# Block products of two token blocks in one set: 512 columns each, with an order of their own for h, gates and second products

## The chip, the cores and the metric

The kernel runs on one core of one Trainium2 chip. Its time is the device time of one launch in microseconds (us), the median of several runs; smaller is better.

## The reference, cut to what matters

Sparse attention over 2 batches of 8 heads (768 tokens, 64 wide) gives x, 1536 tokens by 512. Two feed-forward layers follow, and they are most of the work:

```python
def _moe_ref(x, w_in, w_out):          # first layer
    h = x @ w_in                       # 1536x512 @ 512x2048
    g = h * np.cos(h)
    return g @ w_out                   # 1536x2048 @ 2048x512

def _moe2_ref(x, w_in, w_out):         # second layer, on the first one's result
    h = x @ w_in
    relu6 = np.clip(h + 3.0, 0.0, 6.0)
    g = h * relu6 / 6.0
    return g @ w_out
```

All inputs are float32, and so is the result.

## The kernel before, in words

**Precision.** TensorE multiplies in a reduced form of float32. Each operand is therefore split into a high and a low part ("hi", "lo"), and each product is made of three: hi with hi, lo with hi, hi with lo. The weights are split on the chip (carry, rebias, shift, sign, join, then hi and lo, in `nearest`, `convert` and `convert_pair`), and so are x and g.

**Tiling.** The 1536 tokens are three blocks of 512 (0, 1, 2). A feed-forward layer's 2048 inner columns are 16 slices of 128. For a slice and a block there is first h (128 inner columns on the partitions, 512 tokens in the free dimension), then the gate work (`middle`: turns, rest, cosine, gate in the first layer; relu and gate six in the second; then g hi and g lo), then the second product (`mm2`, 12 matmuls of 512 columns) that adds into four accumulator banks in PSUM. After the last slice of a run of slices, `close` adds the four banks into `total` ("sums", on VectorE where the sum is not the first). The slices are worked in groups (`GROUPS`), each group for the three blocks in turn.

**h in two ways.** The slices 0 to 5 of the first layer are computed directly (`mm1`, line 990). All others come two slices at a time from `mm1_set` (line 923, matmuls at line 941): the product of a 2 by 2 weight block matrix with a 2 by 2 token block matrix is formed from seven block products and not eight. The four weight blocks are two slices by two halves of the depth; sums of them (s1 to s4) come from `convert_pair` and lie in `phi`, `plo`. The four token blocks are two halves of the depth by the two halves (256 tokens each) of one token block; sums of them ("tees") come from `tees` and `tees_of_parts` and lie in `tx`. A block product is six matmuls: three parts by two halves of 128 in depth. One set uses three banks x, y and w of a ring of four (`LATE_H`), and moves each product out of PSUM with "take" (a copy, line 521) or "add" (line 954, VectorE) into tiles `hs`. Four times in a set a product goes into a bank that an add (three times) or a take (once) must have read first.

**Order.** The program is recorded as a list of operations with their dependencies (`Graph.op`). `QUEUES`, a table of numbers at the head of the file, gives every operation an engine and a place in the engine's queue; engines work their queues in that order. `Graph.replay` estimates times only to merge the queues and to place filler matmuls (`fill`, line 1078) where PE would be idle. So a new table moves nearly every instruction.

**Names in the rows.** PE: line 941 is a block product, line 990 a direct h product, line 1108 a second product. DVE is VectorE: line 954 add, 1146 sums, 1068 g lo, 1064 gate six, 1055 rest, 1059 gate, 598/600/602 weight conversion, 538 lo parts of the weights, 851/864/869 tees and their lo parts, 1158 low part of the first layer's result. `hs`, `ch_c` hold h and the gate's tiles; `ghi`, `glo` are g; `total`, `totak` the results; `bank_...` are PSUM banks. POOL is GpSimd, ACT is ScalarE.

```python
def product(o, ok, a, t, first=False, wait=0.0):   # before: bh, bl are 256 columns of one block
    ...
    for n, (wt, xt) in enumerate(((phi, bh), (plo, bh), (phi, bl))):
        for kk in range(2):
            nc.tensor.matmul(
                o, wt[i][:, A[a], kk * P:(kk + 1) * P], xt[:, kk, :], ...
```

Of the kernel before, what the change touches and what calls it, by code (L numbers as in the profile page):

```python
# [11 lines left out]
F32 = mybir.dt.float32  # L12
# [20 lines left out]
def wstart(w, seq):  # L33
# [5 lines left out]
        4 18 19 26 27 35 36 77 43 44 52 53 79 66-68 86 87 69-71 103 94 105 82 96 99 112 121 123 114 381 369-371  # L39
        117 393 394 372 373 382 383 395 396 130 374 397 398 384 385 132 386 149 135 151 405 158 439 160 406 440  # L40
        421 407 408 422 409 163 441 410 423 442 443 424 425 176 444 419 167 178 169 426 181 417 420 418 433 457
        434 436 458 200-205 459-462 438 185 211 187 435 437 491 213 492 493 453 494 216 451 454 452 473 495 474
# [3 lines left out]
        566 568 570 286 573 571 574 572 594-597 606-608 598 609 654 599 610 618 611 655 656 619 620 657 621 622  # L46
        658 623 659 678-681 704-707 682 667 683 666 708 709 749 765 750 766 668 751 767 752-754 669 768 691 693
        690 769 695 735 692 770 694 734 733 783 736 784 785 763 786 787 762 788 829 830 761 831 764 777 779 863
        781 778 845 822 780 846 832 821 833 847 782 834 824 848 842 823 849 850 841 857 864 859 865 861 866 867
        907 844 868 843 929 858 860 915 862 908-910 927 931 916 917 953 918 934 954 956 932 955 936 939 957 967  # L50
# [272 lines left out]
def attention_two_ffn(  # L323
# [30 lines left out]
    HALF = TOK // 2  # L354
    NHB = 2
    GROUPS = ((3, 3, 4, 2, 4), (4, 4, 4, 4))
    BACKWARD = ((0, 0, 0, 1, 1), (1, 0, 1, 0))
    WHOLE = GROUPS[0][0] + GROUPS[0][1]
    plan = []
    for m in range(2):  # L360
# [977 lines left out]
```

## Time and profile before

| | |
|---|---|
| median of 3 runs | 584.77 us (583.97 to 584.91) |
| the profiled execution's own time | 584.38 us |
| span of its trace, first to last instruction | 582.5 us |
| PE busy | 574.1 us (99% of the span), 4303 matmuls in the trace |
| weight loads, DVE, ACT, POOL busy | 508.7, 495.0, 350.6, 209.6 us |
| granted PE clock | 1.000 in the whole span |
| chain that ended last | PE 93%, DVE 4%, DMA, ACT, issue and POOL 1% each |

[...] The attention runs until about 99 us, mixed with the first direct products; from about 100 to 154 us PE has direct and second products alone, and from 154 to 570 us block products and second products; the rest is the last second products and the stores.

### The profile page before, as it was taken

The numbers are of one execution on the slowest core, as the hardware profiler recorded it, in microseconds if no ns is written. First come the engines' busy times: TensorE is split into PE (matmuls) and PEld (weight loads), VectorE is DVE, ScalarE is ACT, GpSimd is POOL, SyncE is SP. The second block draws the span as 40 slices with busy tenths as digits, with TensorE's granted clock in tenths as the row PEclk, the third lists the DMA queues.
The fourth block names the chain that finished last, engine by engine and source line by source line (L and its number), as shares of the span: only waits on it lengthen the run. The fifth ranks groups of instructions, "written<-read, shape, count | busy, mean of one in ns | idle before, by whom it ended". The sixth has DMA issues, their size and how long they took to land.

```text
span 582.5 us, 11210 instructions
## 1 busy us (share of the span) xinstructions
PE 574.1 (99%) x4303; PEld 508.7 (87%) x4303; DVE 495.0 (85%) x975; ACT 350.6 (60%) x768; POOL 209.6 (36%) x203
## 2 busy tenths in 40 slices
PE   9999999999999999999999999999999999999997
PEld 7788889888899888889879898899998989898985
DVE  6998898988988989999899999988988888875644
ACT  5899998777565576757657767754673354231110
POOL 5586655433533342253524531203114004023130
PEclk9999999999999999999999999999999999999999
DMA  8996543212022112331210211321222230200014
GB/s 305 288 279 209 166 145 100 74 36 73 0 74 74 38 71 74 109 109 38 74 36 1 73 58 52 110 73 72 74 73 73 80 109 30 72 1 1 1 55 163
DMA packets 17093, 51.58 MB, mean 89 GB/s; under 512 B 1936, under 2 KB 2192, under 8 KB 17040
## 3 DMA queue, kind: packets, MB, share of 16 engines
q1 hardware_dynamic: 17040, 50.86, 26.2%
q8 instruction: 34, 0.56, 0.4%
q14 instruction: 19, 0.16, 0.1%
HBM read 47.71 MB, written 3.15 MB: 87 GB/s over the span
## 4 chain that ended last, share of the span: by engine, by line
PE 93%; DVE 4%; DMA 1%; ACT 1%; issue 1%; POOL 1%; SPq 0%; DVEq 0%
PE bank_a L1108 24%; PE bank_d L941 17%; PE bank_c L1108 10%; PE bank_b L1108 10%; PE bank_c L941 8%; PE bank_e L941 8%; PE bank_d L990 4%; PE bank_e L990 2%; PE bank_b L793 2%; PE bank_b L809 2%; PE bank_c L990 1%; PE bank_c L730 1%; DMA ktile<-in_kt_dram 1%; PE bank_d L1078 1%; DVE totak L1146 1%; PE bank_c L713 1%
## 5 line engine op out<-in xcount | busy, mean ns | idle before, releaser
L1062 ACT ACTIVATE ch_c<-hs,three 128x512 f32<-128x512 f32 x48 | 34.0, 721 | 64.8 <-DVE hs L954 60.8
L1068 POOL TENSOR_TENSOR glo<-ch_c,ghi 128x512 fp32r<-128x512 f32 x26 | 35.1, 1355 | 74.9 <-ACT ghi L521 33.5
L954 DVE TENSOR_TENSOR hs<-bank_d,hs 128x256 f32<-128x256 f32 x100 | 41.8, 420 | 16.5 <-PE bank_d L941 15.4
L602 POOL TENSOR_TENSOR cv_y<-cv_t,cv_y 128x512 int32<-128x512 int32 x23 | 33.3, 1451 | 58.5 <-DVE cv_t L600 43.4
L521 ACT CAST ghi<-ch_c 128x512 fp32r<-128x512 f32 x63 | 38.9, 620 | 16.0 <-DVE ch_c L1064 8.7
L600 DVE SCALAR_TENSOR_TENSOR cv_t<-raw,cv_t 128x512 int32<-128x512 int32 x64 | 45.1, 705 | 0.2
L1068 DVE TENSOR_TENSOR glo<-ch_c,ghi 128x512 fp32r<-128x512 f32 x58 | 43.1, 746 | 0.7 <-ACT ghi L521 0.6
L593 ACT ACTIVATE cv_t<-raw 128x512 f32<-128x512 f32 x55 | 36.8, 673 | 10.9 <-DVE plo L538 2.9
L583 ACT ACTIVATE cv_y<-raw 128x512 int32<-128x512 uint32 x58 | 38.6, 675 | 5.8 <-DVE wlo_out L538 2.4
L1064 DVE SCALAR_TENSOR_TENSOR ch_c<-ch_c,hs 128x512 f32<-128x512 f32 x48 | 33.2, 698 | 3.7 <-ACT ch_c L1062 3.6
L1053 ACT ACTIVATE ch_c<-hs,quarter 128x512 int32<-128x512 f32 x30 | 21.4, 722 | 21.6 <-DVE hs L954 18.7
L1057 ACT ACTIVATE ch_c<-ch_c,half_pi 128x512 f32<-128x512 f32 x37 | 26.3, 721 | 12.3 <-DVE ch_c L1055 11.9
L941 PE MATMUL bank_d<-xhi,phi 128*128 128x256 f32 x156 | 31.2, 281 | 1.2 <-DVE hs L954 1.2
L941 PEld LDWEIGHTS bank_d<-xhi,phi 128*128 128x128 f32 x156 | 27.2, 189 | 5.5 <-DVE hs L954 1.6
L941 PE MATMUL bank_d<-xhi,plo 128*128 128x256 f32 x156 | 31.4, 282 | 0.0
L941 PE MATMUL bank_d<-xlo,phi 128*128 128x256 f32 x156 | 31.3, 282 | 0.0
L954 DVE TENSOR_TENSOR hs<-bank_e,hs 128x256 f32<-128x256 f32 x47 | 19.8, 421 | 13.3 <-PE bank_e L941 12.8
L598 DVE TENSOR_SCALAR cv_t<-cv_t 128x512 int32<-128x512 int32 x64 | 28.3, 446 | 0.8 <-ACT cv_t L593 0.7
L602 DVE CUSTOM_DVE_ANT_0 cv_y<-cv_t,cv_y 128x1024 uint16<-128x1024 uint16 x41 | 28.6, 705 | 0.3 <-ACT cv_y L583 0.2
L954 DVE TENSOR_TENSOR hs<-bank_c,hs 128x256 f32<-128x256 f32 x48 | 20.1, 418 | 9.1 <-PE bank_c L941 8.6
L763 ACT ACTIVATE es<-bank_c,nmx 128x120 f32<-128x120 f32 x80 | 27.5, 370 | 0.2
L771 POOL TENSOR_TENSOR es<-es,rs 128x960 f32<-128x960 f32 (+1 forms) x13 | 21.4, 1649 | 12.1 <-DVE rs L770 9.9
(367 smaller groups left out, 1978.2 us busy)
## 6 DMA issues: line engine op xcount, KB each, us to landing
raw<-in_w_in_dram SPq DMA_DIRECT2D x32, 512.0 KB, 3.6
raw<-in_w_out_dram SPq DMA_DIRECT2D x32, 512.0 KB, 3.6
vcats<-in_vw_dram SPq DMA_DIRECT2D x12, 384.0 KB, 5.7
qt<-in_q_dram SPq DMA_DIRECT2D x12, 256.0 KB, 5.1
ktile<-in_kt_dram SPq DMA_DIRECT2D x7, 384.0 KB, 5.3
total<-in_vw_dram SPq DMA_DIRECT2D x8, 256.0 KB, 4.9
out_dram<-total SPq DMA_DIRECT2D x8, 256.0 KB, 2.2
vnat<-in_vw_dram SPq DMA_DIRECT2D x4, 256.0 KB, 6.4
```

The source lines that it names most:

```text
L521: nc.scalar.copy(o, i) if e == "ACT" else VEC[e].tensor_copy(o, i)
L583: nc.scalar.activation(y, low.bitcast(U32), AF.Copy, scale=2.0 ** -29)
L593: nc.scalar.activation(o, a, AF.Copy, scale=2.0 ** -112)
L600: G.op("sign", {"DVE": dve(DM)}, lambda e: nc.vector.scalar_tensor_tensor(t, high, -0x80000000, t, ALU.bitwise_and, ALU.bitwise_or), r=[rk ...
L602: G.op("join", {"POOL": pool(DM), "DVE": dve(DM)}, lambda e: VEC[e].tensor_tensor(y, t, y, ALU.add), r=[tk], w=[yk], twice=True)
L941: nc.tensor.matmul(o, wt[i][:, A[a], kk * P:(kk + 1) * P], xt[:, kk, :], start=first and n + kk == 0, stop=n + kk == 3, skip_group_check=True)
L954: G.op("add", {"DVE": dve(HALF)}, lambda e: nc.vector.tensor_tensor(o[0](), a, b[0](), ALU.add), r=[ak, b[1], "room"], w=[o[1]])
L990: nc.tensor.matmul(h, w["in"][i][:, kk * P:(kk + 1) * P], x[blk][:, kk, c0:c1], start=p + kk == 0, stop=p == 2 and kk == NK - 1)
L1062: G.op("relu", {"ACT": act(N) + 0.1}, lambda e: nc.scalar.activation(c(), h(), AF.Relu, bias=three), r=hk, w=ck)
L1064: G.op("gate six", {"DVE": dve(N)}, lambda e: nc.vector.scalar_tensor_tensor(c(), c(), 6.0, h(), ALU.min, ALU.mult), r=hk, w=ck, twice=boo ...
L1068: G.op("g lo", {"DVE": dve(N), "POOL": pool(N)}, lambda e: VEC[e].tensor_tensor(gbuf("lo", s)[:, 0:N], c(), gh().bitcast(F32), ALU.subtrac ...
L1108: nc.tensor.matmul(acc(s, i)[0], l, r, start=first, stop=end and p == 2 and (N == TOK or i % 2 == 1), skip_group_check=N < TOK)
```

## The change

It does five things.

1. The token blocks 0 and 1 are put into one set (`SIDE = [[0, 1], [2]]`): the two columns of the token block matrix are then block 0 and block 1, 512 tokens each (`WIDE = [512, 256]`). Block 2 keeps sets of its own, with halves of 256. All block products, adds and takes of a two-block set work on 512 columns.
2. The sums of token blocks are made for both blocks together, for each 128 of depth in turn (`chunks`), in `tees(0)` after block 1's last result of the first layer and in `tees_of_parts(0, ...)` before the first sets; block 2 has `tees(1)`. The upper half of block 1's result is no longer split by itself, since only sums that contain it are used.
3. From the first set on, an explicit list (`work`) sets what is recorded in which order: a two-block set, the second products left from block 2 of the group before, a second two-block set, then second products and sets of block 2 in turn. The gate work of a slice is recorded as soon as a g tile is free. `BACKWARD`, by which the last block of a group was the first of the next, is gone; with it the four places where a block's accumulators were kept open from one group to the next.
4. h and the gate share one pool of seven tiles (`tile_of`, `assign`).
5. V's block means are copied from PSUM in one operation of four copies, on one engine, and no longer in four operations. The table `QUEUES` is new.

The diff, cut to its core (the table's rows are left out, as are some lines of `tees` that only follow the new indices):

```diff
     GROUPS = ((3, 3, 4, 2, 4), (4, 4, 4, 4))
-    BACKWARD = ((0, 0, 0, 1, 1), (1, 0, 1, 0))
...
-            n = LATE_H[(SETS - NEARLY + (s - SETS) // 2 * 3 + k) % 4]
+            n = LATE_H[(SETS - NEARLY + s - SETS + k) % 4]
+            return bank[n], n
...
+            def put(e):
+                for c in range(P // BLK):
+                    hs = slice(c * CC // D, (c + 1) * CC // D)
+                    copy(e, vcat[0][WK:KC, :, hs, :], bank[mb][BLK * c:BLK * c + NB, 0:CC].rearrange(
+                        "n (h d) -> n h d", d=D).unsqueeze(1).to_broadcast([NB, 2, CC // D, D]))
+
+            G.op("put v", {"ACT": 4 * act(2 * CC), "DVE": 4 * dve(2 * CC)}, put, r=[mb], w=every)
...
+    SIDE = [[0, 1], [2]]
+    WIDE = [TOK, HALF]
+
+    def chunks(z):
+        return (0, 1) if z == 0 else (None,)
+
+    def quarter_of(x, z, k, t, c=None):
+
+        if z == 0:
+            return x[t][:, 2 * k:2 * k + 2, :] if c is None else x[t][:, 2 * k + c, :]
+        return x[SIDE[1][0]][:, 2 * k:2 * k + 2, t * HALF:(t + 1) * HALF]
...
-    def mm1_set(s, due):
+    def mm1_set(z, rows, number, due):
...
-        (x, xk), (y, yk), (w, wk) = (hbank(s, k) for k in range(3))
-        x, y, w = (z[:, 0:HALF] for z in (x, y, w))
+        n = WIDE[z]
+        (x, xk), (y, yk), (w, wk) = (hbank(SETS + 3 * number, k) for k in range(3))
+        x, y, w = (v[:, 0:n] for v in (x, y, w))
...
-            G.op("block product", {"PE": 6 * mm(HALF)}, go, r=[("phi", i, AK[a]), ("plo", i, AK[a]), *xr], w=[ok], due=late[0])
+            G.op("block product", {"PE": 6 * mm(n)}, go, r=[("phi", i, AK[a]), ("plo", i, AK[a]), *xr], w=[ok], due=late[0])
...
         def add(o, a, ak, b):
-            G.op("add", {"DVE": dve(HALF)}, lambda e: nc.vector.tensor_tensor(o[0](), a, b[0](), ALU.add),
-                 r=[ak, b[1], "room"], w=[o[1]])
+            G.op("add", {"DVE": dve(n)}, lambda e: nc.vector.tensor_tensor(o[0](), a, b[0](), ALU.add),
+                 r=[ak, *b[1], "room"], w=o[1])
...
+            z = next(z for z in range(2) if blk in SIDE[z])
+            n = TOK if i >= NK // 2 or blk == SIDE[0][0] else (HALF if z else 0)
...
+            if i == NK - 1 and blk == SIDE[z][-1]:
+                tees(z)
...
+                work += sets(0, pairs[0]) + left
+                if len(pairs) > 1:
+                    work += sets(0, pairs[1])
+                left = seconds(2, range(f0, f0 + n))
+                if m == 0 and f0 + n == NF:
+                    work += seconds(0, range(f0, f0 + n)) + seconds(1, range(f0, f0 + n))
+                    work += [x for f in pairs for x in sets(1, f)] + left
+                    left = []
+                else:
+                    for f in pairs:
+                        work += seconds(0, two(f)) + sets(1, f)
+                    work += seconds(1, range(f0, f0 + n))
```

What it moves is read from the order of instructions in the two programs. First PE in the second half of the second layer's first group, before: block products of 256 columns (two matmuls to a row) between second products of 512.

```order
L1108 MATMUL bank_a0_93<-ghi3_1653,whj_out0_1643 128x512
L1108 MATMUL bank_a0_93<-ghi3_1653,wlj_out0_1645 128x512
L1108 MATMUL bank_a0_93<-glo3_1657,whj_out0_1643 128x512
L1108 MATMUL bank_b_95<-ghi3_1653,whj_out0_1643 128x512
L1108 MATMUL bank_b_95<-ghi3_1653,wlj_out0_1645 128x512
L1108 MATMUL bank_b_95<-glo3_1657,whj_out0_1643 128x512
L1108 MATMUL bank_a1_94<-ghi3_1653,whj_out0_1643 128x512
L1108 MATMUL bank_a1_94<-ghi3_1653,wlj_out0_1645 128x512
L1108 MATMUL bank_a1_94<-glo3_1657,whj_out0_1643 128x512
L941 MATMUL bank_d0_98<-xhi2_87,phi1_70 128x256 x2
L941 MATMUL bank_d0_98<-xhi2_87,plo1_72 128x256 x2
L941 MATMUL bank_d0_98<-xlo2_90,phi1_70 128x256 x2
```

And PE after the change, where the first layer ends and the second layer's first two-block set begins: ten block products of block 2 (256 columns; the last three are shown), the first block product of 512 columns, then second products.

```order
L944 MATMUL bank_d0_98<-xhi2_87,phi0_69 128x256 x2
L944 MATMUL bank_d0_98<-xhi2_87,plo0_71 128x256 x2
L944 MATMUL bank_d0_98<-xlo2_90,phi0_69 128x256 x2
L944 MATMUL bank_d1_99<-xhi2_87,phi0_69 128x256 x2
L944 MATMUL bank_d1_99<-xhi2_87,plo0_71 128x256 x2
L944 MATMUL bank_d1_99<-xlo2_90,phi0_69 128x256 x2
L944 MATMUL bank_c1_97<-xhi2_87,phi0_69 128x256 x2
L944 MATMUL bank_c1_97<-xhi2_87,plo0_71 128x256 x2
L944 MATMUL bank_c1_97<-xlo2_90,phi0_69 128x256 x2
L944 MATMUL bank_e_100<-xhi0_85,phi1_70 128x512 x2
L944 MATMUL bank_e_100<-xhi0_85,plo1_72 128x512 x2
L944 MATMUL bank_e_100<-xlo0_88,phi1_70 128x512 x2
```

In the whole program the 1638 matmuls of 256 columns in block products became 546 of 512 and 546 of 256; the 1080 second products of 512 columns, the direct products and the attention's matmuls are as many as before, and 25 filler matmuls stand where 26 stood, all in the attention.

DVE at the end of the first layer, before: the closing sums of the last block (totak), a weight conversion, the last g lo parts, and the adds (line 954) of a set of the block worked before.

```order
L1146 SCALAR_TENSOR_TENSOR totak0_1658<-bank_b_95,totak0_1658 128x512
L1146 SCALAR_TENSOR_TENSOR totak0_1658<-bank_a1_94,totak0_1658 128x512
L1146 SCALAR_TENSOR_TENSOR totak0_1658<-bank_c0_96,totak0_1658 128x512
L600 SCALAR_TENSOR_TENSOR cv_t1_84<-raw1_68,cv_t1_84 128x512
L1068 TENSOR_TENSOR glo1_1655<-ch_c1_1648,ghi1_1651 128x512
L1158 TENSOR_TENSOR xlo2_90<-totak0_1658,xhi2_87 128x256
L1068 TENSOR_TENSOR glo2_1656<-ch_c2_1649,ghi2_1652 128x512
L954 TENSOR_TENSOR hs0_1665<-bank_d1_99,hs0_1665 128x256
L954 TENSOR_TENSOR hs0_1665<-bank_e_100,hs0_1665 128x256
```

DVE at the same place after the change: the closing sums of block 1, sums of token blocks (line 880) and low parts (line 1179) between the adds (line 960) of the ten block products shown above.

```order
L1165 SCALAR_TENSOR_TENSOR total1_92<-bank_c0_96,total1_92 128x512
L880 TENSOR_TENSOR total1_92<-total1_92 128x512
L960 TENSOR_TENSOR ch_c1_1647<-bank_d1_99,ch_c1_1647 128x256
L960 TENSOR_TENSOR ch_c1_1647<-bank_e_100,ch_c1_1647 128x256
L880 TENSOR_TENSOR total0_91<-total0_91,total1_92 128x512
L960 TENSOR_TENSOR hs1_1663<-bank_d0_98,ch_c0_1646 128x256
L960 TENSOR_TENSOR ch_c1_1647<-bank_d1_99,ch_c1_1647 128x256
L1179 TENSOR_TENSOR xlo1_89<-total1_92,xhi1_86 128x512
L960 TENSOR_TENSOR ch_c0_1646<-bank_d0_98,ch_c0_1646 128x256
L1179 TENSOR_TENSOR xlo1_89<-total1_92,xhi1_86 128x512
L1074 SCALAR_TENSOR_TENSOR hs3_1665<-ch_c1_1647,hs3_1665 128x512
L960 TENSOR_TENSOR ch_c0_1646<-bank_d1_99,ch_c0_1646 128x256
```

After these come the rest of the gate work of block 2's four slices (twelve instructions), sums of token blocks and their low parts (twelve with those shown; three more sums are on POOL), one low part of weights, three steps of weight conversion, two closing sums of block 2, and the first two adds of the two-block set. From the first add shown to the second of these two it is 43 DVE instructions: nine adds of 256 columns, one weight shift, and 33 others of 512. Over the whole program, DVE's adds go from 195 of 256 columns to 65 of 256 and 65 of 512, its sums from 68 to 84, and its other groups change by a few each.

## Rows read from the trace of the kernel before

**Rows 1.** The page: busy time of each engine; the granted PE clock.

```profile
PE 574.1 (99%) x4303; PEld 508.7 (87%) x4303; DVE 495.0 (85%) x975; ACT 350.6 (60%) x768; POOL 209.6 (36%) x203
PEclk9999999999999999999999999999999999999999
```

**Rows 2.** Stretches (start:end, length, busy (count)): PE, PEld, DVE, ACT, POOL, clock.

```profile
0.00:100.00 100.00, 96.85 (x1439) 83.76 (x1440) 85.53 (x190) 87.13 (x291) 62.35 (x81) 1.00 0.66 212
...
280.00:300.00 20.00, 18.84 (x114) 16.42 (x114) 18.59 (x31) 11.85 (x22) 7.11 (x6) 1.00 0.17 54
...
334.00:571.00 237.00, 237.00 (x1485) 213.99 (x1484) 191.19 (x388) 106.69 (x197) 52.86 (x50) 1.00 0.18 62
```

**Rows 3.** The same stretches: matmuls of line 941 alone, then of line 1108 alone.

```profile
334.00:571.00 237.00, 127.92 (x942) 125.35 (x940) 1.00 0.18 62
...
334.00:571.00 237.00, 141.09 (x543) 95.71 (x544) 1.00 0.18 62
```

**Rows 4.** Chain that ended last (start, us, what): direct products of 512 columns.

```profile
100.49 4.11 PE bank_d L990 x18
...
111.40 3.63 PE bank_d L990 x16
```

**Rows 5.** The same chain: block products of 256, second products of 512.

```profile
399.60 1.42 PE bank_d L941 x12
...
567.11 1.82 PE bank_a L1108 x8
...
570.33 0.93 PE bank_a L1108 x4
```

**Rows 6.** What PE waited for after 155 us: total, times, longest.

```profile
PE bank_d L941 <- DVE hs L954: 1.2, 1, 1.2
PE bank_d L941 <- ACT ch_c L1062: 0.3, 1, 0.3
```

**Rows 7.** Timeline of PE around the two waits (start, us, engine line op).

```profile
292.18 0.40 PE L1108 MATMUL bank_b<-glo,whi_out 128*128 128x512 f32 x1
293.74 0.50 PE L941 MATMUL bank_d<-xhi,phi 128*128 128x256 f32 x2 [1.16 <-DVE hs L954]
...
332.27 0.39 PE L1108 MATMUL bank_c<-glo,whi_out 128*128 128x512 f32 x1
333.00 0.47 PE L941 MATMUL bank_d<-txhi,phi 128*128 128x256 f32 x2 [0.34 <-ACT ch_c L1062]
```

**Rows 8.** Timeline of DVE before the first wait.

```profile
288.33 0.69 DVE L1146 SCALAR_TENSOR_TENSOR totak<-bank_c,totak 128x512 f32<-128x512 f32 x1
...
289.54 1.78 DVE L1068 TENSOR_TENSOR glo<-ch_c,ghi 128x512 fp32r<-128x512 f32 x1
...
291.58 1.77 DVE L1068 TENSOR_TENSOR glo<-ch_c,ghi 128x512 fp32r<-128x512 f32 x1
293.27 0.41 DVE L954 TENSOR_TENSOR hs<-bank_d,hs 128x256 f32<-128x256 f32 x1
```

**Rows 9.** Timeline of POOL in the same 10 us.

```profile
289.10 1.67 POOL L851 TENSOR_TENSOR totak<-totak 128x512 f32<-128x512 f32 x1 [0.24 <-DVE totak L1146]
291.45 1.34 POOL L1158 TENSOR_TENSOR xlo<-totak,xhi 128x512 fp32r<-128x512 f32 x1 [0.68 <-ACT xhi L521]
```

**Rows 10.** Timeline of DVE: full queue; an add right behind its product.

```profile
271.62 0.68 DVE L1068 TENSOR_TENSOR glo<-ch_c,ghi 128x512 fp32r<-128x512 f32 x1
272.22 0.42 DVE L954 TENSOR_TENSOR hs<-bank_c,hs 128x256 f32<-128x256 f32 x1
272.55 0.42 DVE L598 TENSOR_SCALAR cv_t<-cv_t 128x512 int32<-128x512 int32 x1
...
570.37 0.42 DVE L954 TENSOR_TENSOR hs<-bank_d,hs 128x256 f32<-128x256 f32 x1 [0.35 <-PE bank_d L941]
```

**Rows 11.** Groups of instructions: count | busy us, mean ns | idle before.

```profile
L1078 PE MATMUL bank_d<-zero 128*128 128x512 f32 x25 | 6.7, 406 | 0.0
L521 DVE COPY vcats<-bank_e 24x256 f32<-24x256 f32 x4 | 1.7, 423 | 0.4 <-PE bank_e L661 0.3
```

More of the change, by code (lines that the diff above doesn't have):

```diff
@@ L834, in attention_two_ffn @@
     NH = 4
[L835 removed]
+    LENT = (1, 0)
     PAUSE = 0.3
[L838 to L875 removed]
@@ new lines, in tees, with keys, two @@
+    def tees(z):
+        n = 2 * HALF
+        for c in chunks(z):
+            b11, b12, b21, b22 = (lambda k=k, t=t, c=c: quarter_of(total, z, k, t, c) for k in range(2) for t in range(2))
+            def keys(k, t):
+                ks = (2 * k, 2 * k + 1) if c is None else (2 * k + c,)
+                return [("total", t if z == 0 else SIDE[1][0], kk) for kk in ks]
+            k11, k12, k21, k22 = (keys(k, t) for k in range(2) for t in range(2))
+            def two(op, o, x, y, r, w):
+                G.op("tees", {"POOL": pool(n), "DVE": dve(n)}, lambda e: VEC[e].tensor_tensor(o(), x(), y(), op),
+                     r=[*r, "room"], w=w, twice=True)
+            two(ALU.subtract, b12, b22, b12, k22, k12)
+            tee_parts(z, 2, c, b12, k12)
+            two(ALU.add, b11, b11, b12, k12, k11)
+            tee_parts(z, 1, c, b11, k11)
+            two(ALU.subtract, b21, b21, b11, k11, k21)
+            tee_parts(z, 3, c, b21, k21)
+            two(ALU.subtract, b22, b22, b11, k11, k22)
+            tee_parts(z, 0, c, b22, k22)
@@ L1231, in attention_two_ffn @@
     pending = []
-    for s in range(NSTEP):
+    for s in range(SETS):
         if s == NEARLY:
@@ L1247, in attention_two_ffn, with sets, seconds, two @@
+        while pending and pending[0] <= s - lag:
             events.append(("second", pending.pop(0)))
-    events += [("second", r) for r in pending]
+    step = {(m, b, f): s for s, (m, b, f, _, _) in enumerate(plan) if s >= SETS}
+    work = [("second", r) for r in pending]
+    left = []
+    for m in range(2):
+        f0 = 0
+        for g, n in enumerate(GROUPS[m]):
+            if step.get((m, 0, f0)) is not None:
+                pairs = list(range(f0, f0 + n, 2))
+                def sets(z, f):
+                    rows = [[step[m, b, f + j] for j in range(2)] for b in SIDE[z]]
+                    s_rows[rows[0][0]] = rows
+                    return [("set", rows[0][0], z)]
+                def seconds(b, fs):
+                    return [("second", step[m, b, f]) for f in fs]
+                def two(f):
+                    return (f, f + 1)
+                work += sets(0, pairs[0]) + left
[5 more added lines that the diff above has]
+                    work += [x for f in pairs for x in sets(1, f)] + left
+                    left = []
+                else:
+                    for f in pairs:
+                        work += seconds(0, two(f)) + sets(1, f)
+                    work += seconds(1, range(f0, f0 + n))
+            f0 += n
@@ new lines, in attention_two_ffn @@
+    work += left
+    slots, made = NG1 - len(pending), set()
+    queue = [x[1] for x in work if x[0] == "second" and x[1] >= SETS]
+    for x in work:
+        events.append(x)
+        if x[0] == "second":
+            slots += 1
+        else:
+            made.update(y for r in s_rows[x[1]] for y in r)
+            if x[2] == 1:
+                events += [("used", y) for r in s_rows[x[1]] for y in r]
+        while queue and slots and queue[0] in made:
+            events.append(("middle", queue.pop(0)))
+            slots -= 1
@@ L1249, in attention_two_ffn @@
     assign()
-    now = 0
-    for what, s in events:
+    now, cursor, number = 0, when(SETS), 0
+    for what, s, *z in events:
         m, b, f, _, _ = plan[s]
         n = slices.index((m, f))
-        G.late = 3 if s >= SETS else (2 if what == "switch" else max(G.late, 1))
+        inset = bool(z) or s >= SETS
+        G.late = 3 if inset else (2 if what == "switch" else max(G.late, 1))
         if what == "switch":
```

274 lines of the change are left out of this document (131 added, 143 removed), and 194 rows, old and new, of the table QUEUES.

## The prediction

> **What bounds the kernel now.** I read the page first: PE is busy 99% of the span at full granted clock, no other engine over 85% [rows 1]. So the time is what PE's queue costs plus PE's few waits. The second view is the stretches: from 334 to 571 us PE has no idle time at all, and 942 matmuls of 256 columns and 543 of 512 fill the 237 us exactly [rows 2, 3]. The third is the list of PE's waits: after 155 us there are two, 1.2 and 0.3 us [rows 6]. Only two things can then make the late part faster: fewer or cheaper matmul steps, and those two waits. DVE is the engine that could become the next bound, since it is busy 18.59 of 20 us from 280 to 300 us [rows 2].
>
> **Cost of a step.** A row's busy time overlaps its neighbour's, so I use distances between starts. 512 columns alone in the queue: 34 direct products in 4.11 + 3.63 us, 0.2276, and the second piece alone 0.2269 [rows 4]; second products far from block products 1.82/8 = 0.2275, right behind them 0.93/4 = 0.2325 [rows 5]. 256 columns: 1.42/12 = 0.1183 inside a run [rows 5]. So a 512 step behind a run of 256 steps costs more than elsewhere, and part of the price of 256 columns is paid by the neighbour. The stretch from 334 to 571 us holds all of it: with 0.2267 for each of the 543 wide steps, (237 - 123.1)/942 = 0.1209 us for a narrow one. Two narrow steps then cost 0.2418, one wide 0.2267.
>
> **1. Wide steps.** 1638 narrow matmuls become 546 wide and 546 narrow, so 546 times a pair becomes one. 546 x 0.0151 = 8.2 us gained. Lower bound: the cheapest pair of rows, 2 x 0.1183, against the dearest wide step, 0.2325: 0.0041 x 546 = 2.3 us. Upper bound: there are far fewer changes between narrow and wide steps, so the 546 narrow steps that stay may cost 0.119 and not 0.1209, 1.0 us more: 9.2. I take 8.2, since the stretch of rows 3 is the full mix of the late part. All of it lies on PE, the path that sets the end.
>
> **2. The two old waits go.** 292.18 to 293.74 is 1.56 us for a step of 0.23, 332.27 to 333.00 is 0.73 [rows 7]: 1.33 + 0.50 = 1.8 us. Both are at places where the order is new, so I take them out and judge the new order by itself. The first one's cause is instructive. PE waited for an add (line 954) [rows 6]; ahead of it in DVE's queue stood two g lo of 1.78 and 1.77 us, where a g lo in a full queue is 0.68 and the next begins 0.60 after it [rows 8, 10]. Each of the two overlaps a POOL instruction, and ends 0.55 us after that one's end (290.77 to 291.32, 292.79 to 293.35) [rows 8, 9]: they stood still until POOL was done, and cost 1.1 us each. [...]
>
> **3. DVE's load.** In a full queue a 512 instruction takes 0.60 and a 256 one 0.335 from start to start [rows 10]. Adds: 195 x 0.335 = 65.3 us become 65 x 0.335 + 65 x 0.60 = 60.8. Sums: 16 more, since no block's accumulators stay open over two groups, 9.6 us. Net 5 us more on an engine with 495 of 582.5 us busy. It costs nothing where PE has slack over DVE, so the question is where it has none.
>
> **4. The end of the first layer.** That is the place. Before, three blocks ended apart and each had its sums of token blocks made beside another block's products. Now block 0 waits for block 1, and 24 instructions for both (sums, high and low parts) come due at once, beside ten narrow products of block 2 in a row, whose adds PE needs promptly, and the gate work of four slices. From the first of these adds to the second add of the first wide set DVE has 33 x 0.60 + 10 x 0.335 = 23.2 us. PE's work between the same two points is 8 narrow products (6 x 0.12), 5 wide ones and 48 second products' matmuls: 8 x 0.72 + 5 x 1.36 + 48 x 0.2267 = 23.4 us. There is no slack: each time POOL holds a DVE instruction there, PE will wait. POOL has five or six instructions there (sums, low parts, a weight join). With two holds as in rows 8, 2.2 us. In the run of ten products a bank comes again after one other product (0.72 us); the add begins 0.04 after the product's last matmul, takes 0.42, and PE starts 0.06 later [rows 5, 7, 8, 10], 0.52 together, so an add that stands behind one other DVE instruction is late; I put 1.0 us for three or four such. Sum 3.2 us. Ends: 0.5 (no hold, and one late add) and 6 x 1.1 + 2.0 = 8.6.
>
> **5. The rest at nothing.** V's means in one operation: four copies of 0.42 [rows 11] before and after, on ACT and not on DVE the first time; other work of the attention covers them, and 1.7 us is the price if none does. The attention's order is new too: PE idles or runs fillers there (25 of them, 6.7 us [rows 11]; 96.85 of 100 us busy [rows 2]), so a new table could win or lose about 1 us: 0, with 1 us either way. The end is the same code, second products, two sums, stores. The weights' conversion is the same work with more time between a pair's last use and its successor's first.
>
> **Sum,** against the profiled execution's 584.38 us (its trace spans 582.5; the median of runs, 584.77, is 0.07% above, which I neglect): 584.4 - 8.2 - 1.8 + 3.2 + 0 = **577.6 us**. All gains with no costs: 584.4 - 9.2 - 1.8 + 0.5 - 1 = 572.9. All costs: 584.4 - 2.3 - 1.8 + 8.6 + 1 = 589.9.
>
> **Rivals.**
>
> A. No new wait of note. Term 4 is 0.5 and the rest as above: 574.9 (573 to 576 with term 1's upper end). For it: a table searched for this order can put POOL's instructions where they hold no one. Against it: the first wait of before arose at the same place, with one block's sums to make there and not two.
>
> B. DVE saturates at the end of the first layer: term 4 is 8.6, 583.0. For it: 23.2 against 23.4 us. [...]
>
> C. A wide step is no cheaper than its columns: it costs 0.2325 everywhere, as behind block products in rows 5, and a pair 2 x 0.1183. Gain 2.3 and not 8.2: 583.5. Against it: direct products of 512 columns stand at 0.2269 for 16 in a row [rows 4]. [...]
>
> D. Slower: exposed drains. A wide set has three products that follow in a bank which an add must first read, and that add of 512 columns takes 0.69 (the sums' row, also from PSUM [rows 8]), with 0.04 and 0.06 about it 0.79 us. 13 wide sets have 39 such places; if all were exposed, 30.8 us: 608. It passes 585.9 from about 11 of them on, and with half of them it is 593. Against it: in the new order at least one other wide product (1.36 us) lies between any two of the same bank. For it: that covers the add only if DVE takes it within 0.57 us, and its neighbours in the queue take 0.60.
>
> That the change does not do what it says I exclude: the order shows 546 wide and 546 narrow matmuls.
>
> **How the numbers follow.** Forecast (576 to 580) 0.58; A 0.17; B (580 to 583.5) 0.12; C, with other mixtures that end near the old time, 0.08; D 0.05. The likeliest is 577.6. A measurement of this kernel can tell about 0.2% from no change, 1.2 us. Faster by more (under 583.6): forecast, A and B, 0.87; within 0.2%: C, 0.08; slower: D, 0.05. The range 573.5 to 583.0 leaves out the far end of A, and C and D.
>
> **What the new profile would show.** Right: 13 x 42 wide block product matmuls at 0.227 from start to start, second products behind them at 0.227 and not 0.2325; PE's list of waits headed by an add and a g lo within 30 us of the first layer's end, 2 to 5 us in sum, with DVE instructions of over 1 us beside POOL's in front of them. Wrong in term 1: wide steps of 0.232. Wrong in term 4: waits spread over all groups (D), or none (A). Wrong in term 5: the first direct-product stretch without attention beginning more than 1 us away from 100 us.

## The result: 576.04 us, and the profile after

The changed kernel took 576.04 us, median of four runs (574.94 to 577.43), beside 584.84 for the kernel before: a ratio of 0.985, 95% interval 0.983 to 0.988. The forecast was 577.6, the range 573.5 to 583.0. Two later measurements gave the changed kernel 575.59 (six runs) and 575.33 (six). Of these 16 runs, the six over 576 us (576.85 to 581.48) are the six whose mean granted clock is 0.997 or less; the other ten, 573.98 to 575.91 us, have a median of 574.9. The profiled run is the slowest of the first four, 577.43 us with a span of 575.7.

The page of the changed kernel, the two lines that answer to [rows 1], and three stretches, as in [rows 2]:

```profile
PE 566.1 (98%) x3756; PEld 481.9 (84%) x3756; DVE 493.2 (86%) x922; ACT 349.9 (61%) x750; POOL 204.6 (36%) x197
PEclk8999999999999999999999999999999999999999
```

```profile
0.00:100.00 100.00, 95.01 (x1395) 81.68 (x1396) 83.37 (x191) 84.12 (x288) 61.98 (x78) 0.98 0.68 212
300.00:320.00 20.00, 19.28 (x113) 16.86 (x112) 19.59 (x35) 12.80 (x24) 7.53 (x5) 1.00 0.00 0
334.00:564.00 230.00, 230.00 (x1173) 196.99 (x1172) 189.22 (x353) 107.30 (x188) 54.12 (x51) 1.00 0.18 61
```

PE has 547 matmuls fewer. From 334 us on it is still busy all the time. New are two things: at 300 to 320 us DVE is busy 19.59 of 20 us, and in the first 100 us PE is busy 95.0 and not 96.9, at a mean clock of 0.98.

The chain that ended last (start, us, what), answering to [rows 4, 5]; L944 is the block product, L1127 the second product:

```profile
376.78 1.36 PE bank_d L944 x6
...
408.54 1.44 PE bank_d L944 x12
...
368.59 0.93 PE bank_a L1127 x4
369.98 2.72 PE bank_a L1127 x12
```

From start to start a wide step costs 1.36/6 = 0.2267 and a narrow one 1.44/12 = 0.120; the trace's record of one is 0.39 and 0.28 us long, so neighbours overlap. Four second products right behind narrow steps still take 0.93, 0.2325 each, and twelve in a row 0.2267.

Of the waits after 155 us the list names one. The second is too short for the list, but stands in PE's timeline (start, us, engine line op):

```profile
PE bank_d L944 <- DVE hs L960: 0.6, 1, 0.6
```

```profile
307.53 0.40 PE L944 MATMUL bank_d<-xlo,phi 128*128 128x256 f32 x2
308.56 0.51 PE L944 MATMUL bank_d<-txhi,phi 128*128 128x256 f32 x2 [0.63 <-DVE hs L960]
...
311.30 0.40 PE L944 MATMUL bank_d<-xlo,phi 128*128 128x256 f32 x2
311.79 0.51 PE L944 MATMUL bank_d<-xhi,phi 128*128 128x256 f32 x2
```

From start to start these two places cost 0.79 and 0.25 us more than steps, 1.0 us in all; with one slow step behind each, 1.3. Both are among the ten narrow products of block 2 at the end of the first layer, where the prediction put them. The old two [rows 7] are gone. DVE and POOL there:

```profile
307.28 0.89 DVE L880 TENSOR_TENSOR total<-total,total 128x512 f32<-128x512 f32 x1
308.10 0.41 DVE L960 TENSOR_TENSOR hs<-bank_d,ch_c 128x256 f32<-128x256 f32 x1
308.43 0.41 DVE L960 TENSOR_TENSOR ch_c<-bank_d,ch_c 128x256 f32<-128x256 f32 x1
308.76 1.10 DVE L1179 TENSOR_TENSOR xlo<-total,xhi 128x512 fp32r<-128x512 f32 x1
309.79 0.41 DVE L960 TENSOR_TENSOR ch_c<-bank_d,ch_c 128x256 f32<-128x256 f32 x1
...
310.72 0.68 DVE L1074 SCALAR_TENSOR_TENSOR hs<-ch_c,hs 128x512 f32<-128x512 f32 x1
311.32 0.41 DVE L960 TENSOR_TENSOR ch_c<-bank_d,ch_c 128x256 f32<-128x256 f32 x1
```

```profile
305.83 1.79 POOL L880 TENSOR_TENSOR total<-total,total 128x512 f32<-128x512 f32 x1
307.58 1.73 POOL L529 TENSOR_TENSOR plo<-cv_y,phi 128x512 fp32r<-128x512 f32 x1
```

The add that PE waited for (308.10) stood behind a subtraction of the tees, itself held to 0.89 us beside POOL. The low part of y at 308.76 took 1.10 and ended 0.55 us after POOL's instruction (309.31 to 309.86): the hold of [rows 8, 9] again. In both traces every DVE instruction that took over 0.08 us more than the median of its line and form (37 before, 30 after) overlaps an instruction of POOL. The adds and sums, one input of which is PSUM, are not among them: none of the 263 before and 214 after takes more than 0.43 us (256 columns) or 0.69 (512), though 146 and 130 of them overlap an instruction of POOL.

### The profile page after: what moved, and what is told of

It reads as the page before. It is cut to its first block, busy times and chain, and to the rows that moved or that the text cites. A ratio compares the mean times of both kernels' runs of the same rounds, so it can differ in the third digit from the quotient of the medians.

```text
span 575.7 us, 10041 instructions
## 1 busy us (share of the span) xinstructions
PE 566.1 (98%) x3756; PEld 481.9 (84%) x3756; DVE 493.2 (86%) x922; ACT 349.9 (61%) x750; POOL 204.6 (36%) x197
## 4 chain that ended last, share of the span: by engine, by line
PE 93%; DVE 4%; DMA 1%; issue 1%; ACT 0%; POOL 0%; SPq 0%; POOLq 0%; DVEq 0%
PE bank_a L1127 24%; PE bank_d L944 15%; PE bank_b L1127 11%; PE bank_c L1127 10%; PE bank_e L944 9%; PE bank_c L944 9%; PE bank_d L996 4%; PE bank_e L996 2%; PE bank_b L786 2%; PE bank_b L802 2%; PE bank_c L996 1%; PE bank_c L723 1%; PE bank_d L1097 1%; DMA ktile<-in_kt_dram 1%; PE bank_c L706 1%
## 5 line engine op out<-in xcount | busy, mean ns | idle before, releaser
L512 ACT CAST ghi<-hs 128x512 fp32r<-128x512 f32 x45 | 27.8, 619 | 21.8 <-DVE hs L1083 12.7
L1087 DVE TENSOR_TENSOR glo<-hs,ghi 128x512 fp32r<-128x512 f32 x47 | 33.2, 708 | 1.6 <-ACT ghi L512 1.0
L589 DVE TENSOR_SCALAR cv_t<-cv_t 128x512 int32<-128x512 int32 x64 | 26.8, 422 | 1.3 <-ACT cv_t L584 1.0
L1087 POOL TENSOR_TENSOR glo<-ch_c,ghi 128x512 fp32r<-128x512 f32 x9 | 13.0, 1439 | 39.5 <-ACT ghi L512 32.2
L944 PE MATMUL bank_d<-xhi,phi 128*128 128x256 f32 (+1 forms) x106 | 26.3, 330 | 0.1
L512 ACT CAST ghi<-ch_c 128x512 fp32r<-128x512 f32 x28 | 17.3, 619 | 14.8 <-DVE ch_c L1083 6.7
L944 PE MATMUL bank_d<-xlo,phi 128*128 128x256 f32 (+1 forms) x106 | 26.2, 329 | 0.0
L944 PE MATMUL bank_d<-xhi,plo 128*128 128x256 f32 (+1 forms) x106 | 26.2, 329 | 0.0
L1165 DVE SCALAR_TENSOR_TENSOR total<-bank_a,total 128x512 f32<-128x512 f32 x28 | 19.0, 685 | 3.1 <-PE bank_a L1127 3.1
L944 PEld LDWEIGHTS bank_d<-xhi,phi 128*128 128x128 f32 x106 | 18.8, 189 | 3.2 <-DVE ch_c L960 0.3
L1127 PE MATMUL bank_a<-ghi,whi_out 128*128 128x512 f32 x60 | 21.3, 389 | 0.0
L1127 PE MATMUL bank_a<-ghi,wlo_out 128*128 128x512 f32 x60 | 21.3, 389 | 0.0
```

What stands on the lines that cost most here:

```text
L512: nc.scalar.copy(o, i) if e == "ACT" else VEC[e].tensor_copy(o, i)
L589: G.op("shift", {"DVE": dve(DM, 2)}, lambda e: nc.vector.tensor_scalar(t, t, 3, None, ALU.logical_shift_left), w=[tk], twice=True)
L944: nc.tensor.matmul(o, wt[i][:, A[a], kk * P:(kk + 1) * P], xt[:, kk, :], start=first and p + kk == 0, stop=p + kk == 3, skip_group_check=True)
L1087: G.op("g lo", {"DVE": dve(N), "POOL": pool(N)}, lambda e: VEC[e].tensor_tensor(gbuf("lo", s)[:, 0:N], c(), gh().bitcast(F32), ALU.subtrac ...
L1127: nc.tensor.matmul(acc(s, i)[0], l, r, start=first, stop=end and p == 2 and (N == TOK or i % 2 == 1), skip_group_check=N < TOK)
```

## The experiments

Theory: the 8 to 9 us are the width of the steps, little else is left, and what the profiled run lost in the attention is its new start. Rivals: the order alone, or a VectorE that is full at the end of the first layer.

**1. The width undone.** Wide products as two times six narrow steps:

```
-   for p, (wt, xt) in enumerate(((phi, bh), (plo, bh), (phi, bl))):
-       for kk in range(2): matmul(o, ..., xt[:, kk, :], start=first and p + kk == 0, ...)
+   for c in range(0, n, HALF):
+       for p, (wt, xt) in enumerate(((phi, bh), (plo, bh), (phi, bl))):
+           for kk in range(2): matmul(o[:, c:c + HALF], ..., xt[:, kk, c:c + HALF], start=first and c + p + kk == 0, ...)
```

> The changed kernel, but each wide product of blocks 0 and 1 (512 columns) is issued as two times six steps of 256 columns into the two halves of its bank, as it was before; queues, tees, adds and banks stay those of the change. Theory (the gain is the width of the step: 2 x 0.119 of the narrow against 0.227 of the wide in a row, and the 0.229 to 0.236 of the second products right behind narrow steps): the block products grow by 546 x (0.238 - 0.227) = 6 us, the mean of a second product goes from 0.2274 back towards 0.2320, some 3 to 5 us over 1079, and the time is 8 to 10 us over the changed kernel, 584 to 586 us. First rival (only the row of block products gains, the second products are faster for their order): 6 us, 582. Second rival (the width saves nothing, the gain is in the order and in fewer waits): within 1.5 us of the changed kernel, 575 to 577.

Measured: 582.73 us (582.29 to 583.25), 7.2 over the changed kernel with longer zeros (575.53) measured beside it. The wait of the end of the first layer is the same (first row), and from the attention's last product to the first block product it is 59.3 us in both kernels, so nothing else moved; the next rows are the chain of this kernel, products and second products behind them:

```profile
PE bank_d L951 <- DVE hs L967: 0.6, 1, 0.6
```

```profile
341.04 1.43 PE bank_d L951 x12
...
366.78 0.93 PE bank_b L1134 x4
```

The steps from start to start, over the whole late part (sums over all PE records of each trace; waits are in them, and stand in a line of their own as what they cost above a step, as in the prediction's second term):

| | before | halves | changed |
|---|---|---|---|
| block products, us | 195.0 | 197.1 | 190.4 |
| 1079 second products of 512, us | 250.3 | 246.5 | 245.4 |
| together | 445.3 | 443.6 | 435.8 |
| of these, waits | 1.8 | 1.0 | 1.0 |
| changes from narrow to wide steps | 172 | 81 | 33 |
| wide steps above 0.2267, sum, us | 3.9 | 1.9 | 0.9 |

The width is worth 7.8 us of steps, 7.2 of time; the order alone 1.7, of which 0.8 is less waiting. The time lies between the theory and its first rival, nearer the rival: the block products grew by 6.7 us, but of the 3 to 5 us that the theory put on the second products only 1.1 came. The last two lines show what the price of narrow steps is made of: behind a change the first five wide steps have medians of 0.233, 0.236, 0.228, 0.232 and 0.231, later ones 0.227, in all three kernels. That is 0.022 to 0.028 us a change. The first narrow step behind a wide one is in turn a little cheaper, 0.114 where it is 0.120 inside a run. The new order alone halves the number of changes and so gains 2.0 us on the second products; 1.1 of them are lost again on narrow steps.

**2. The old start.** All queues up to the attention in the order of before, what comes later as changed.

> The changed kernel with everything up to the attention (and the direct first and second products, which stand in the same stretch) in the order of the kernel before, the means of V written by four operations again; all that comes later as changed. Theory (the new start of the attention costs 2 to 3 us where the clock falls): the clock stays full from 6.2 us on, the last product of the attention ends at 99 us and not at 101.5, and the time is 573.5 to 575.0 us, with runs that lie within 1 us. Rival (the new order of the attention is worth something by itself, and its start only moves work that is hidden): 577 us or more. If the start is nothing either way: 576.0.

Measured: 582.25 us (581.81 to 582.97). Neither theory nor rival: the two halves don't fit. A wait of 4.2 us arose at a place that neither kernel has, in the direct products, and PE stood most of 110 to 115 us:

```profile
PE bank_d L1001 <- DVE ch_c L1083: 4.2, 1, 4.2
```

```profile
110.00:115.00 5.00, 1.36 (x7) 0.78 (x5) 5.00 (x9) 3.36 (x7) 2.65 (x2) 1.00 0.12 48
```

By putting all later work behind the attention in each queue I had put gates behind DVE's weight work, which both kernels mix. The granted clock of 100 to 160 us was 0.97, where the run with longer zeros has 1.00. The stretch between the attention's last product and the first block product took 65.4 us where it takes 59.3 in the changed kernel, so all of the loss is there. About the start the time says nothing; the profile has the attention's last product at 99.7 us, inside the range of the changed order's profiles at full clock (98.6 to 100.0, below).

**3. Longer zeros ahead of the scores.** In the profile of the changed kernel PE waits for the first keys, and the granted clock of the two stretches behind is 0.82 and 0.84, where before it was 1.00 (PE timeline, then stretches as in [rows 2], changed and before):

```profile
7.42 0.35 PE L720 MATMUL bank_c<-ktile,qt 64*64 64x96 f32 x2 [1.26 <-DMA ktile<-in_kt_dram]
8.32 0.30 PE L721 MATMUL bank_c<-ksum,qt 64*64 64x24 f32 x1 [0.55 <-DVE ksum L617]
```

```profile
5.00:10.00 5.00, 3.19 (x40) 2.48 (x39) 3.38 (x8) 0.39 (x1) 0.76 (x2) 0.82 1.00 388
10.00:15.00 5.00, 5.00 (x77) 3.89 (x77) 3.65 (x10) 3.05 (x15) 0.22 (x1) 0.84 0.60 225
```

```profile
5.00:10.00 5.00, 4.94 (x50) 3.68 (x48) 4.18 (x9) 1.68 (x9) 1.61 (x3) 1.00 0.98 373
10.00:15.00 5.00, 4.71 (x108) 3.92 (x108) 3.78 (x13) 4.63 (x23) 2.22 (x5) 1.00 0.91 327
```

```
- G.op("wake", {"PE": 0.43 * WAKE}, lambda e: wake(WAKE), ...)
+ G.op("wake", {"PE": 0.43 * WAKE}, lambda e: wake(WAKE + 6), ...)
```

> The changed kernel with 17 instead of 11 of the products of zeros that TensorE does before its first real ones; nothing else. In the profile of the changed kernel TensorE waits 1.26 us for the first keys (to 7.42) and 0.55 us for their maxima (to 8.32), and the clock is at half from 8.2 to 11.6 us. Theory (idle TensorE before the scores lets the clock fall): with six more products, 1.3 to 2.6 us of work, the clock stays full, the last attention product ends near 99 us, and the time is 574 to 575 us. Rival (the clock falls for what comes after, not for the idle stretch, or the attention is bound by its loads): the products of zeros only push the scores back, 576 us or up to 1 us more.

> The changed kernel once more, beside the three below on the same chip. Its first four runs were 574.94 to 577.43 us, and the mean granted clock of them 1.000 to 0.996. Theory (the spread is the start): the runs spread by 1.5 us or more again, and where the profile shows TensorE idle between its first products and the first scores, the granted clock falls to half for some 3 us. Rival (the spread is noise of the whole run): the clock is full everywhere and the runs still spread so.

> The changed kernel with 17 products of zeros, once more: 575.67 us (574.79 to 576.04) in its first five runs, where the changed kernel had 575.59 (574.75 to 580.64). Theory (longer zeros buy nothing in an undisturbed run and keep out the runs with a fallen clock): 575.0 to 576.0 again, no run over 577 and no mean clock under 0.998. Rival (chance): one run or more over 577 us with a mean clock of 0.997 or less.

Measured: 575.67 (574.79 to 576.04) and 575.53 (575.29 to 577.08) with longer zeros; the changed kernel beside the first, the control, 575.59 (574.75 to 580.64). In the profile with longer zeros the clock is full (1.00 from 0 to 50 us), the attention's last product ends at 99.0 us (before 98.9, changed 101.5), and the span is 573.0. The median did not move: zeros gain nothing there. They don't settle the spread either: one of their own runs took 577.08 us at full clock. And my theory had the place of the fall wrong: in the control's profile the clock is full at the start (1.00 from 0 to 20 us), and the loss (its attention ends at 104.7 us) came later, between 20 and 30 us:

```profile
25.45 0.80 PE L786 MATMUL bank_b<-ident,es 128*120 128x128 f32 x3 [2.98 <-issue]
```

```profile
25.00:30.00 5.00, 4.55 (x35) 3.15 (x38) 0.91 (x2) 2.44 (x15) 1.11 (x1) 0.51 0.38 92
```

PE stood 2.98 us in the middle of four transposes with nothing to wait for that the profile shows, and then had half the clock (0.51 in 25 to 30 us).

Where runs differ can be read from the profiles together. With the changed order it is 59.3 us from the attention's last product to the first block product in every one of them (but the old start), and 411.0 us from there to PE's last product in every one whose late part is not edited. So the changed kernel's runs differ in the attention alone (the stop is PE's idle time, as in the row above; the other columns are us from the span's start):

| profile | the stop, us | clock at half | attention ends |
|---|---|---|---|
| before | 0.55 | never | 98.9 |
| changed | 1.48 | 8.2 to 11.6 | 101.5 |
| control (changed again) | 2.98 | 25.1 to 31.9 | 104.7 |
| changed, a third time | 2.47 | never | 100.0 |
| halves | 1.14 | never | 98.6 |
| longer zeros | 1.06 | never | 99.0 |
| longer zeros again | 1.60 | never | 99.5 |
| four copies, longer zeros | 2.05 | 24.2 to 27.7 | 102.4 |

In the changed order at full clock the attention ends at 98.6 to 100.0 us, latest behind the longest stop; with some 3.4 us at half clock at 101.5 to 102.4, with 6.8 at 104.7. So the profiled run's 2.6 us are in the main its fallen clock (3.4 us at half clock are at most 1.7 us of work, an estimate), the rest waits and the stop.

**4. What that stop is.** With six more zeros ahead, the stop is in another operation:

```profile
21.92 0.42 PE L658 MATMUL bank_e<-total,avg 128*32 128x128 f32 x5 [1.06 <-issue]
```

Counted in PE's records, it is behind product 348 in the kernel before (the row below), in the changed one and in all variants but the old start (341) and those with the seven products added below.

```profile
21.24 0.27 PE L661 MATMUL bank_e<-total,avg 128*32 128x128 f32 x1 [0.55 <-issue]
```

A packet of 16 KB of an instruction queue begins 2.4 to 2.9 us ahead of its end in each: at 18.79, 22.64, 22.60 and 19.39 us, and PE goes on at 21.24, 25.09, 25.45 and 21.92 (before, changed, control, longer zeros). I take the queue for PE's: it has 34 packets of 16 KB in the trace of before and 29 in that of the changed kernel, where PE has 547 products and as many weight loads fewer. So I put seven products of zeros about ten instructions ahead of the stop:

```
  after[i] = max(0, int((begins[j] - ends[i] - 0.3) / mm(512)))
+ after[84] += 7          # 84: scores of the sixth unit
```

> The changed kernel a third time, as the measure for the two below. In nine profiles of the changed kernel and its variants TensorE stands still once between 20 and 26 us, for 0.8 to 3.3 us, with no semaphore to wait for, and always behind its 348th product (341st in one), whichever operation that is; a 16 KB packet of the instruction queue starts 2.4 to 2.9 us ahead of its end. Theory (TensorE has run out of instructions, and how long depends on the loads that the packet stands behind): the same stop behind product 348, and runs between 574.7 and 578 us, the longer ones at a mean clock of 0.997 or less. Rival (a data wait that the profile doesn't show): the stop at the same operation, L786, but at another number.

> The changed kernel with 17 products of zeros at the start, and seven more such products of 512 columns (1.6 us) between the scores of the sixth unit and the transposes behind them, some ten products ahead of the place where TensorE stands still at 21 to 25 us. Nothing else. Theory (the stop is a fetch of instructions that takes 2.4 to 2.9 us from its packet's start, asked for before the seven): the stop behind product 348 shrinks by up to 1.6 us, the seven products lie in time that was idle, the clock stays full from 16 to 30 us, and the runs lie within 1 us of each other at 574.5 to 575.5 us. Rival (the seven products are only more work on a full engine): the stop keeps its length, 1.1 to 2.3 us, and the time is 1.6 us more, 577.

The stop of the changed kernel measured beside it (timeline, then the instruction queue in 20 to 23 us: packets, MB, share), and the same place with the seven products:

```profile
20.83 0.32 PE L786 MATMUL bank_b<-ident,es 128*120 128x128 f32 x1
23.62 0.49 PE L786 MATMUL bank_b<-ident,es 128*120 128x128 f32 x3 [2.47 <-issue]
```

```profile
q8 instruction: 1, 0.02, 2.8%
```

```profile
20.52 1.89 PE L1104 MATMUL bank_d<-zero 128*128 128x512 f32 x7
22.25 0.60 PE L793 MATMUL bank_d<-ident,es 128*120 128x128 f32 x4
22.78 1.14 PE L659 MATMUL bank_e<-total,avg 128*32 128x128 f32 x16
```

Measured: PE's idle time behind product 348 shrinks from 2.47 to 0.10 us (from start to start, 2.79 to 0.37). The four runs lie between 576.09 and 576.35, where the changed kernel's six beside them lie between 573.98 and 581.48 (median 575.33). As to the cause the theory holds as far as these runs go: place by count, a packet of instructions ahead of its end, and a stop that shrinks by what is put in front of it. In the third order of experiment 6, which has the same zeros, the packet began at 19.29 us and not at 21.06, and there is no stop at all. That PE had run out of instructions is the reading that fits all of it; no row shows what PE holds. The forecast time, 574.5 to 575.5, was missed: the median is 0.9 over the changed kernel's. Whether the seven products cost that is open, since it lies within the other's spread; nor is it shown that they narrow the spread, since the third order's four runs, with the same seven, lie between 575.84 and 577.51. Why the packet starts late is not shown either: the DMA engines are full then (share 0.97 of 20 to 25 us), but they are in the kernel before, too (0.95), whose packet came earliest, and no run took loads away.

**5. Means of V by four operations again,** on top of the longer zeros.

> The changed kernel with 17 products of zeros, and the means of V written by four operations again, one behind the other at the place where the one operation stands. The instructions on the engine are the same four copies; only what may stand between them and the waits on them differ. Theory (the one operation changes nothing): the same as with 17 products of zeros alone, within 0.6 us. Rival (its four copies of 1.5 us in a row hold ScalarE ahead of the exponentials of the scores, and TensorE's transposes wait for these): with four, the first of the readers start earlier and the time falls by 0.5 to 1 us.

Measured: 576.03 us (574.75 to 578.82) against 575.53 (575.29 to 577.08): no difference beyond the spread. At nothing, as predicted.

**6. Three other orders of VectorE at the end of the first layer.** The numbers are operations in DVE's queue: 1539, 1542, 1584, 1541, 1589, 1592, 1544, 1591 adds; 1519, 1522 tees; 1506, 1503 low parts of y; 1570, 1572, 1574 rest, gate and low part of one gate.

```
  changed  1519 1539 1542 1522 1584 1541 1506 1589 1503 1570 1592 1544 1591 1572 ...
  first    1519 1539 1542 1584 1541 1522 1589 1506 1592 1503 1544 1591 1570 1572 ...
  second   1519 1539 1542 1584 1541 1522 1589 1570 1592 1544 1591 1506 1572 1503 1574 ...
  third    1519 1539 1542 1584 1541 1522 1589 1506 1592 1570 1503 1544 1591 1572 ...
```

> The changed kernel with two places of VectorE's queue reordered: at the end of the first layer, the adds of the ten narrow products of block 2 go ahead of one subtraction of the tees, two low parts of y and one middle step that stood between them. Nothing else moves. Theory (TensorE's two late waits there, 0.79 us before 308.56 and 0.25 us before 311.79 with the slow products behind them some 1.3 us in all, are work queued ahead of the adds): both waits fall under 0.15 us, and the time is 0.8 to 1.3 us under the changed kernel on the same chip. Rival (VectorE is the bound of the whole stretch): the waits come back in the stretch behind, 312 to 330 us, and the time is the same within 0.4 us.

The first: 577.31 us (575.89 to 578.76), 1.7 over its control. Both old waits went, and PE stood 2.06 us for a gate's rounded part, with the clock at 0.66 in the stretch behind (wait, DVE, stretch):

```profile
PE bank_c L1133 <- ACT ghi L518: 1.9, 1, 1.9
```

```profile
310.18 1.40 DVE L1080 SCALAR_TENSOR_TENSOR hs<-ch_c,hs 128x512 f32<-128x512 f32 x1
312.38 0.69 DVE L1084 TENSOR_TENSOR hs<-ch_c,hs 128x512 f32<-128x512 f32 x1 [0.79 <-ACT hs L1082]
```

```profile
315.00:320.00 5.00, 5.00 (x16) 3.94 (x16) 5.00 (x9) 4.50 (x9) 0.00 (x0) 0.66 0.00 0
```

The gate's first step had moved behind the adds and took 1.40 us there, where the next of its line took 0.68 (at 313.32); by its length it was held. From the first block product to PE's last it is 414.1 us in this profile, where the changed order has 411.0.

> The changed kernel with 17 products of zeros, and another order of VectorE at the end of the first layer: the adds of the ten narrow products ahead of one subtraction of the tees and two low parts of y, as in the first such try, but with the chain rest, cosine, gate, rounded and low part of the gate (which the second products behind wait for) kept at its place or earlier. Theory (the 2.06 us that the first try lost came from that chain alone, held behind the adds, and the two waits of 0.79 and 0.25 us can be had back): both old waits under 0.15 us, no new wait over 0.3 us between 300 and 335 us, and 0.8 to 1.3 us under the kernel with 17 products of zeros. Rival (VectorE is full there and only the place of the wait can be chosen): a new wait of 0.5 us or more behind the ten products, and the time within 0.4 us or above.

The second: 579.72 us (577.5 to 579.84). The gate's first step now came before ScalarE was done, DVE waited 0.84 us for it, and the adds behind it, and later a low part of the sums of token blocks, came late:

```profile
PE bank_d L950 <- DVE ch_c L966: 0.8, 1, 0.8
PE bank_c L950 <- DVE txlo L870: 0.7, 1, 0.7
PE bank_c L950 <- DVE hs L966: 0.2, 1, 0.2
```

From the first block product to PE's last it is 413.3 us here. The rest of what this profile lost is in the attention: it ends at 101.7 us, behind a stop of 1.70 us and with the clock at half from 23.4 to 26.8 us (stretches):

```profile
20.00:25.00 5.00, 3.30 (x54) 2.48 (x45) 3.94 (x8) 3.52 (x18) 3.79 (x3) 0.84 0.92 270
25.00:30.00 5.00, 5.00 (x75) 3.44 (x75) 2.36 (x6) 3.42 (x19) 1.29 (x2) 0.82 0.31 80
```

> As the one before, and a third order of VectorE's queue at the end of the first layer: one subtraction of the tees moves behind three adds of the narrow products, and one low part of y behind two; the chain rest, cosine, gate begins within 0.2 us of its old time. The first try lost 2.06 us to that chain, the second held an add behind it. Theory (some of the 0.79 and 0.25 us can be had back, what VectorE's load leaves): both waits under 0.2 us, a wait of 0.3 to 0.6 us at the second products behind, and 0.3 to 0.8 us less than the kernel with the seven products. Rival (VectorE is full from 304 to 332 us, so every wait only moves): waits of 0.9 us or more in sum between 300 and 335 us, and no gain.

The third: 576.65 us (575.84 to 577.51) against 576.2 with the seven products and the old order; from the first block product to PE's last it is 411.8. The old waits went, and 0.77 and 0.53 us came at the second products behind:

```profile
PE bank_c L1134 <- ACT ghi L519: 0.6, 1, 0.6
PE bank_c L1134 <- DVE glo L1094: 0.4, 1, 0.4
```

The rival's reading held three times: DVE is full here, and none of the three orders removed the waits; they moved them, and the late part became 0.7 to 3.1 us longer. That no order could do better is not shown. None of these versions beats the changed kernel.

## Why the prediction was right, step by step

The sum was 584.4 - 8.2 - 1.8 + 3.2 + 0 = 577.6. By the trace it is 584.4 - 8.7 - 1.8 + 1.0 = 574.9. The ten runs at full clock have their median there; the medians of all runs, 575.3 to 576.0, leave 0.4 to 1.1 for the attention.

**1, wide steps.** Predicted 8.2 (2.3 to 9.2), measured 8.7: without waits 443.5 us of steps became 434.8, of which the halves put 7.8 down to the width and 0.9 to the order. The reason given for the upper bound is the one that came true, fewer changes between narrow and wide. What I called the price of a narrow step, 0.1209, holds the price of 99 changes: in the 237 us it was read from, the wide steps lie 2.2 us above 0.2267 in sum and the narrow ones about 1 us below 0.120; what is left, some 1 us over 942 steps, is the 0.0009. Rival C is out: wide block products stand at 0.2267, not 0.2325.

**2, the old waits.** Gone, 1.8, as predicted.

**3, DVE's load.** 5 us more were forecast; the page shows 493.2 after 495.0. The extra work is there by the counts (65 adds fewer, half of the 130 that are left twice as wide, and 16 sums more), but held instructions became fewer: what DVE's instructions took above the median of their line and form (over 0.08 us each) sums to 15.9 us before and 10.7 after, 5.2 of the 6.8 that the forecast is off. I hadn't counted that the new table would cut the holds.

**4, end of the first layer.** Right place, right kind, too large: 1.0, with slow steps 1.3, where I took 3.2. The two terms were mis-sized. Holds: four instructions held by 0.95 us in sum between 300 and 325 us, not two by 1.1 each. Late adds: two, not three or four, since the table keeps two adds together (308.10 and 308.43). That there is no slack was right: 19.59 of 20 us, and three tries that only moved the wait. Rival A's price (0.5) was nearer than mine, let alone B's (8.6): A's sum, 574.9, is that of the trace, though by 8.2 and 0.5 and not 8.7 and 1.0. D did not occur: no step between 155 and 300 us or after 320 is late by 0.1 us.

**5, attention.** 0 is right for the runs at full clock. The fallen clock that two of the first four runs had was not in the prediction: the 1.1 of their median can be put down to it, and in the profiled run the attention lost 2.6 us, outside of the 1 allowed. One of its sources stood in the trace of before in small: the stop behind product 348 is there with 0.55 us, as a wait for "issue" that I passed over.

The prediction's error against the median, 1.6 us, is 0.5 of term 1 and 2.2 of term 4, less 1.1 of the attention. That it is no more is luck in part: a wait priced too high stood against a fallen clock that nobody had priced. Against the runs at full clock the error is 2.7 us.

## What to carry to other kernels

Where TensorE's queue is full, price a step from a stretch that holds the whole mix, from start to start, and count the changes between shapes, too. Where an engine is busy 98% of a stretch, expect its order to move waits and not to remove them, as three orders did here: take work from it, or leave the wait where it is shortest. When runs of one kernel spread, find the stretch in which their profiles differ (here the first 100 us alone), and look in it for fallen clock and for a wait for "issue"; count instructions up to it.

## What the hardware showed that was not expected

TensorE stops with nothing to wait for that the profile shows; that it had run out of instructions is my reading. The stop is tied to a count of instructions (behind product 348), not to an operation, and ended 2.4 to 2.9 us after a 16 KB packet of the instruction queue began; it lasted 0.55 us in the kernel before and 1.1 to 3.0 us in the changed one and its variants, and with seven products of 512 columns ahead of it 0.10. It stands in a dense stretch: from 15 to 30 us a product starts 0.014 us after the one before in the median of the kernel before and 0.013 in that of the changed one, nine in ten within 0.12, while the DMA engines are busy 0.70 to 1.00 of each 5 us.

The clock did not follow the length of a stop alone: it fell to half, for 3.4 to 6.8 us, behind stops of 2.98, 2.05 and 1.70 us (control, four copies, second order), and stayed full behind others of 2.47, 1.83 and 1.60 (changed a third time, first order, longer zeros again). And the first wide steps behind narrow ones cost up to 0.01 us more each (medians of 0.228 to 0.236 against 0.227), for five steps; no run here shows why.
